# Windowed attention and two gated layers on one core: masks added on VectorE, weights rebased with one multiplication

## The chip, the cores and the metric

The kernel is one program on 1 core of a Trainium2 chip. The metric is the device time of one execution in microseconds (us).

## The reference, cut to what matters

Attention over 4 batches, 8 heads, 576 positions of 64 numbers; four heads see the last 32 positions, four see every fourth of the last 128. Two dense layers follow, over 2304 rows.

```python
scores = scale * np.matmul(q, k.transpose(0, 1, 3, 2))
scores = np.where(masks[None, :, :, :], scores, -1000000000.0)
scores = scores - np.max(scores, axis=-1, keepdims=True)
attn = np.exp(scores)
attn = attn / (np.sum(attn, axis=-1, keepdims=True) + 1e-09)
x = np.matmul(attn, v)                  # then laid out as 2304 x 512
h = x @ w_in                            # 512 -> 2048
x = (h * np.cos(h)) @ w_out             # 2048 -> 512
gate = 1.0 / (1.0 + np.exp(-(x @ w_gate)))   # 512 -> 1536
out = (gate * (x @ w_val)) @ w_out2     # 1536 -> 512
```

Inputs q, k, v are float32; the weights arrive as float64. The result is float32.

## The kernel before, in words

**Stages.** The first dense layer runs over 6 chunks of 384 rows and 16 slices of 128 hidden columns, 96 steps of 24 matmuls. Slices 0 to 7 go over all chunks first (steps 0 to 47), then slices 8 to 15. A float32 value is split into a rounded part and a remainder, and each product is three matmuls (`mm3`, lines 676 to 680). The second layer takes two chunks at a time, 36 sections, with seven block products for four (lines 960 to 1082). Attention works on 12 groups of 192 rows and 4 head pairs, 48 tiles, and runs beside steps 0 to 36.

**An attention tile** (`attn_tasks`, line 471). q and k are loaded (`load_qk`), turned on TensorE (`transp`), copied from PSUM on VectorE or ScalarE (`q_parts`, `k_parts`), and multiplied (`scores`). A plain tile has 3 blocks of 128 rows (two heads of 64) by 96 keys, a dilated tile 4 blocks of 96 rows by 80 keys. The mask reaches the scores by a matmul: the identity times a bfloat16 mask tile (`mp` or `md`, entries 0 or -2**33, lines 556 and 559) opens the PSUM group, and the score products add to it. `s_max` (line 568) takes each row's maximum. Tiles of the first two groups (`direct`) multiply the maximum by -scale (`s_neg`, line 576) and give it to the exponential as a bias, which then reads PSUM (line 584); the others subtract the maximum into SBUF first (`s_sub`, line 572), and the exponential reads SBUF (line 587). `s_norm` on GpSimd, a transposition, a copy, the product with V and a split into two parts follow. `band` (line 262) makes the masks on GpSimd at the start; a tile's first 32 keys are set by `head` on GpSimd.

**Weights** (`w_tasks`, line 309). A float64 tile of 128x512 is loaded (`wst`, two buffers) and made float32 with integer operations on its two 32-bit halves: `low` (ScalarE, line 332) scales the low half; `mag` clears the sign (VectorE, line 336, or ScalarE, line 340); `clamp` (line 344) takes the maximum with 2**-15; `shift` (line 347) moves left by 3 and masks; `top` (line 350) puts the top two bits back; `rnd` (line 360) adds the low part. `hi` (ScalarE, line 367) rounds to the matmul's format and `lo` (GpSimd, line 371) takes the remainder. Of 68 tiles, 16 belong to slices 0 to 7, 16 to slices 8 to 15, 36 to the second layer.

**The order of work** is written before the run by a planner (`Plan`, line 48): each task has an engine, a duration, inputs, buffers it takes and gives, a priority (the step at which it is due) and sometimes a second engine (`alt`). The planner steps through modelled time and gives each engine the ready task with the least priority; the chip's queues then hold that order. `port=True` keeps a task from running beside another such task (VectorE and GpSimd). `gate` holds a weight load until a step has begun: `W_GATE` names the first step and the step from weight to weight, for slices 8 to 15 and for the second layer. All loads are issued from SP's queue. Until step 0, TensorE is given small matmuls on an identity (`keep_warm`, line 1110).

Of the kernel before, what the change touches and what calls it, by code (L numbers as in the profile page):

```python
# [9 lines left out]
F32 = mybir.dt.float32  # L10
F32R = mybir.dt.float32r
BF16 = mybir.dt.bfloat16
I32 = mybir.dt.int32
# [9 lines left out]
NEG = -(2.0**33)  # L23
INV_2PI = 0.15915494309189535
TWO_PI = 6.283185307179586
HALF_PI = 1.5707963267948966
F64_MIN = 2.0**-15
# [12 lines left out]
W_GATE = (4.413, 1.646, 36.0, 1.7)  # L40
# [137 lines left out]
def windowed_attention_mlp_kernel(ctx, tc, q, k, v, w_in, w_out, w_gate, w_val, w_out2, out):  # L178
# [80 lines left out]
    mp = ac.tile([P, PB + 1, PW], BF16, name="mp")  # L259
# [14 lines left out]
    band(mp[:, 0, :], PW, True)  # L274
    band(mp[:, 1, :], PW, False)
    for i in range(2, PB + 1):
        POOL.tensor_copy(mp[:, i, :], mp[:, 1, :])
    for z in range(2):
        band(md[:, z, :], DW, z == 0)
# [29 lines left out]
    def w_tasks(i):  # L309
# [24 lines left out]
        def mag():  # L334
            st["c"] = wst.tile([P, DM], I32, tag="wc", name="wc")
            DVE.tensor_scalar(st["c"], st["raw"][:, :, 1], 0x7FFFFFFF, None, op0=ALU.bitwise_and)

        def mag_act():
            st["c"] = wst.tile([P, DM], I32, tag="wc", name="wc")
            ACT.activation(out=st["c"].bitcast(F32), in_=st["raw"][:, :, 1].bitcast(F32), func=AF.Abs)  # L340

        def clamp():
            c = st["c"].bitcast(F32)
            DVE.tensor_scalar(c, c, F64_MIN, None, op0=ALU.max)

        def shift():
            DVE.tensor_scalar(st["c"], st["c"], 3, 0x3FFFFFF8, op0=ALU.logical_shift_left, op1=ALU.bitwise_and)

        def top():
            DVE.scalar_tensor_tensor(st["c"], st["raw"][:, :, 1], -0x40000000, st["c"], op0=ALU.bitwise_and,  # L350
                                     op1=ALU.bitwise_or)
# [10 lines left out]
        def hi():  # L362
# [4 lines left out]
            ACT.activation(out=wt[key][:, 0, :], in_=st["c"].bitcast(F32), func=AF.Copy)  # L367
# [795 lines left out]
```

## Time and profile before

| | |
|---|---|
| median of 3 runs | 983.49 us (982.2 to 986.23) |
| profiled execution, its own time | 983.52 us |
| its span | 981.6 us |
| mean granted TensorE clock | 0.988 |
| instructions | 16366 |
| VectorE, mean of the 68 `top` / 68 `shift` / 68 `clamp` operations | 730 / 490 / 461 ns |
| ScalarE, mean of the 32 `hi` / 35 `mag` operations | 627 / 662 ns |

The span runs from the first to the last instruction of one profiled execution. Busy time is the union of an engine's instructions. Matmuls are pipelined and their listed lengths overlap, so TensorE's cost is read from starts. Idle time of an engine that nothing waits for costs nothing.

### The profile page before, as it was taken

To read this page: it belongs to the slowest core of one execution; us is meant where nothing else is said; L and a number is where in the kernel's file an instruction comes from. 1 tells how busy PE (TensorE), PEld (TensorE's weight loads), DVE (VectorE), ACT (ScalarE), POOL (GpSimd) and SP (SyncE) were. 2 spreads that over 40 slices of the span, in tenths; PEclk is the share of its full clock that TensorE was granted. 3 is DMA by queue.
4 is the path that set the end of the run, shared out by engine and by line. 5 is a ranking of instruction groups with operands and counts; after the bars stand their busy time and mean duration, and the time that the engine had idled before them with its cause. 6 is when DMAs were issued, how large, how long until landed. Compare 5 with 4: busy or idle time off the path is not lost.

```text
span 981.6 us, 16366 instructions
## 1 busy us (share of the span) xinstructions
PE 950.2 (97%) x6007; PEld 893.0 (91%) x6007; DVE 688.8 (70%) x1419; ACT 494.8 (50%) x1193; POOL 177.2 (18%) x228
## 2 busy tenths in 40 slices
PE   7889999999999999999999999999999999999996
PEld 6778889989999999999999989999999999999995
DVE  7789998978765987979899587657544645444443
ACT  5778888777665755665675443323312223221122
POOL 6334333223101332222213122100000000000000
PEclk9699999999999999999999999999999999999999
DMA  7565555455320566778758998785644544644441
GB/s 185 147 192 147 183 155 160 134 159 148 74 79 30 193 226 221 282 244 314 248 193 275 331 335 330 252 320 193 213 152 182 188 162 177 239 157 150 151 150 64
DMA packets 107759, 189.80 MB, mean 193 GB/s; under 512 B 56992, under 2 KB 91040, under 8 KB 100512
## 3 DMA queue, kind: packets, MB, share of 16 engines
q1 hardware_dynamic: 107680, 188.77, 56.7%
q8 instruction: 47, 0.77, 0.3%
q14 instruction: 32, 0.26, 0.1%
HBM read 139.98 MB, written 48.76 MB: 192 GB/s over the span
## 4 chain that ended last, share of the span: by engine, by line
PE 73%; DVE 12%; DMA 7%; ACT 6%; issue 2%; SPq 1%; ACTq 0%; DVEq 0%
PE acc L678 5%; PE ps_h L678 5%; PE oacc L1074 5%; PE oacc L1075 5%; PE oacc L1073 5%; PE acc L680 4%; PE acc L679 4%; PE ps_h L680 4%; PE ps_h L679 4%; PE ps_y L988 3%; PE ps_y L990 3%; PE ps_y L989 3%; PE ps_z L990 2%; PE ps_z L989 2%; PE ps_z L988 2%; PE ps_x L988 2%
## 5 line engine op out<-in xcount | busy, mean ns | idle before, releaser
L678 PE MATMUL acc<-gs,arena 128*128 128x384 f32 x384 | 135.3, 352 | 0.0
L678 PE MATMUL ps_h<-arena 128*128 128x384 f32 x384 | 131.8, 343 | 0.2 <-DVE u L738 0.2
L679 PE MATMUL ps_h<-arena 128*128 128x384 f32 x384 | 128.9, 336 | 0.0
L680 PE MATMUL ps_h<-arena 128*128 128x384 f32 x384 | 128.8, 335 | 0.0
L680 PE MATMUL acc<-gs,arena 128*128 128x384 f32 x384 | 128.7, 335 | 0.0
L679 PE MATMUL acc<-gs,arena 128*128 128x384 f32 x384 | 128.6, 335 | 0.0
L436 POOL TENSOR_TENSOR th<-tb,th 128x512 fp32r<-128x512 f32 (+1 forms) x48 | 60.4, 1272 | 185.4 <-ACT th L431 152.9
L1021 ACT ACTIVATE sg<-sg 128x384 f32<-128x384 f32 x36 | 18.9, 525 | 135.9 <-DVE sg L1017 135.9
L1073 PE MATMUL oacc<-arena 128*128 128x512 f32 x216 | 84.5, 391 | 2.4 <-DVE arena L1035 1.9
L1075 PE MATMUL oacc<-arena 128*128 128x512 f32 x216 | 85.5, 396 | 0.0
L1074 PE MATMUL oacc<-arena 128*128 128x512 f32 x216 | 85.5, 396 | 0.0
L728 ACT ACTIVATE r<-ps_h,q 128x384 int32<-128x384 f32 x96 | 55.4, 577 | 58.3 <-PE ps_h L680 55.8
L735 ACT ACTIVATE u<-u,half_pi 128x384 f32<-128x384 f32 x96 | 58.5, 612 | 38.5 <-DVE u L732 37.8
L1006 DVE TENSOR_TENSOR sg<-ps_y,s 128x384 f32<-128x384 f32 x36 | 20.0, 556 | 80.3 <-PE ps_y L990 80.3
L678 PEld LDWEIGHTS ps_h<-arena 128*128 128x128 f32 x384 | 72.4, 188 | 1.5 <-DVE u L738 0.5
L988 PE MATMUL ps_y<-arena 128*128 128x384 f32 x216 | 72.8, 337 | 0.7 <-DVE u L738 0.5
L678 PEld LDWEIGHTS acc<-gs,arena 128*128 128x128 f32 x384 | 72.2, 188 | 0.9
L990 PE MATMUL ps_y<-arena 128*128 128x384 f32 x216 | 72.9, 337 | 0.0
L989 PE MATMUL ps_y<-arena 128*128 128x384 f32 x216 | 72.8, 337 | 0.0
L679 PEld LDWEIGHTS ps_h<-arena 128*128 128x128 f32 x384 | 72.4, 189 | 0.2 <-POOL arena L371 0.2
L680 PEld LDWEIGHTS ps_h<-arena 128*128 128x128 f32 x384 | 72.4, 188 | 0.0
L679 PEld LDWEIGHTS acc<-gs,arena 128*128 128x128 f32 x384 | 72.3, 188 | 0.0
(137 smaller groups left out, 2340.1 us busy)
## 6 DMA issues: line engine op xcount, KB each, us to landing
arena<-wd SPq DMA_DIRECT2D x36, 1792.0 KB, 7.4
wd<-th SPq DMA_DIRECT2D x12, 1792.0 KB, 7.0
wst<-in_moe_w_out_dram SPq DMA_DIRECT2D x28, 512.0 KB, 4.2
wst<-in_moe_w_in_dram SPq DMA_DIRECT2D x16, 512.0 KB, 4.4
xd<-arena SPq DMA_DIRECT2D x4, 1536.0 KB, 6.2
wst<-in_moe_w_gate_dram SPq DMA_DIRECT2D x12, 512.0 KB, 4.3
wst<-in_moe_w_val_dram SPq DMA_DIRECT2D x12, 512.0 KB, 5.4
od<-oh SPq DMA_DIRECT2D x12, 512.0 KB, 6.9
```

What stands on the lines that cost most here:

```text
L436: POOL.tensor_tensor(out=t[:, 1, c], in0=wf[f][:, c].bitcast(F32), in1=t[:, 0, c].bitcast(F32), op=ALU.subtract)
L678: PE.matmul(ps, wh, xl, start=first, stop=False)
L679: PE.matmul(ps, wl, xh, start=False, stop=False)
L680: PE.matmul(ps, wh, xh, start=False, stop=last)
L728: ACT.activation(out=st["r"], in_=st["h"], func=AF.Identity, scale=INV_2PI, bias=q25)
L735: ACT.activation(out=st["u"], in_=st["u"], func=AF.Sin, scale=TWO_PI, bias=half_pi)
L988: PE.matmul(st[to], wh, xl, start=first, stop=False, **more)
L989: PE.matmul(st[to], wl, xh, start=False, stop=False, **more)
L990: PE.matmul(st[to], wh, xh, start=False, stop=kk == 1, **more)
L1073: PE.matmul(ps, ul, w[:, 0, :], start=f == 0, stop=False)
L1074: PE.matmul(ps, uh, w[:, 1, :], start=False, stop=False)
L1075: PE.matmul(ps, uh, w[:, 0, :], start=False, stop=f == F2 - 1)
```

## The change

Masks: no mask matmul; each score product starts its own PSUM region. For every block, one VectorE operation (`tensor_tensor_reduce`) adds the mask, multiplies by -scale, writes the result to SBUF and gives the row's minimum; that is 3 operations for a plain tile and 4 for a dilated one. The exponential then reads SBUF with scale -1 and the minimum as bias, in all tiles, and the scores' PSUM bank is free after the VectorE operations. `mp` shrinks from 4 blocks to 2, and GpSimd's two copies that filled it go.

Weights: `mag` becomes a multiplication of the high half, read as float32, by 2**-112, first choice ScalarE; `clamp` goes; `shift` loses its mask, `top` keeps one bit. `hi` may also run on VectorE.

Order: the first weight loads get a later priority than the first q and k load; k of the first group is issued from ScalarE's queue; `W_GATE` moves from 4.413 and 36.0 to 12.0 and 40.0. The planner's durations for the changed tasks change with them.

```diff
-F64_MIN = 2.0**-15
...
-W_GATE = (4.413, 1.646, 36.0, 1.7)
+W_GATE = (12.0, 1.8, 40.0, 1.7)
...
-    mp = ac.tile([P, PB + 1, PW], BF16, name="mp")
+    mp = ac.tile([P, 2, PW], BF16, name="mp")
...
-    band(mp[:, 0, :], PW, True)
-    band(mp[:, 1, :], PW, False)
-    for i in range(2, PB + 1):
-        POOL.tensor_copy(mp[:, i, :], mp[:, 1, :])
     for z in range(2):
+        band(mp[:, z, :], PW, z == 0)
         band(md[:, z, :], DW, z == 0)
...
-        def mag():
+        def mag(on_dve=False):
             st["c"] = wst.tile([P, DM], I32, tag="wc", name="wc")
-            DVE.tensor_scalar(st["c"], st["raw"][:, :, 1], 0x7FFFFFFF, None, op0=ALU.bitwise_and)
-
-        def mag_act():
-            st["c"] = wst.tile([P, DM], I32, tag="wc", name="wc")
-            ACT.activation(out=st["c"].bitcast(F32), in_=st["raw"][:, :, 1].bitcast(F32), func=AF.Abs)
-
-        def clamp():
-            c = st["c"].bitcast(F32)
-            DVE.tensor_scalar(c, c, F64_MIN, None, op0=ALU.max)
+            c, x = st["c"].bitcast(F32), st["raw"][:, :, 1].bitcast(F32)
+            if on_dve:
+                DVE.tensor_scalar(c, x, 2.0**-112, None, op0=ALU.mult)
+            else:
+                ACT.activation(out=c, in_=x, func=AF.Copy, scale=2.0**-112)
 
         def shift():
-            DVE.tensor_scalar(st["c"], st["c"], 3, 0x3FFFFFF8, op0=ALU.logical_shift_left, op1=ALU.bitwise_and)
+            DVE.tensor_scalar(st["c"], st["c"], 3, None, op0=ALU.logical_shift_left)
 
         def top():
-            DVE.scalar_tensor_tensor(st["c"], st["raw"][:, :, 1], -0x40000000, st["c"], op0=ALU.bitwise_and,
+            DVE.scalar_tensor_tensor(st["c"], st["raw"][:, :, 1], -0x80000000, st["c"], op0=ALU.bitwise_and,
...
-        def hi():
+        def hi(on_dve=False):
             if j < 0:
                 wt[key] = halves(at((i if i < NW else i - NW) * W_SZ, W_SZ))
             else:
                 wt[key] = late["oh"].tile([P, 2, DM], F32R, tag="oh", name="oh")
-            ACT.activation(out=wt[key][:, 0, :], in_=st["c"].bitcast(F32), func=AF.Copy)
+            if on_dve:
+                DVE.tensor_copy(wt[key][:, 0, :], st["c"].bitcast(F32))
+            else:
+                ACT.activation(out=wt[key][:, 0, :], in_=st["c"].bitcast(F32), func=AF.Copy)
...
-        add(("w_load", i), "sp", 1460, load, [], pr - 2 if j + 2 * F1 >= 2 * FN[0] else GS * (i / 4 - 6) + W_START, take=["raw"], lat=2200 if i < 2 * FN[0] else 3200, gate=gate,
+        add(("w_load", i), "sp", 1460, load, [], pr - 2 if j + 2 * F1 >= 2 * FN[0] else max(GS * (i / 4 - 6) + W_START, -GS * (A_LEAD + 1) - QK_LEAD + 0.1), take=["raw"], lat=2200 if i < 2 * FN[0] else 3200, gate=gate,
             after=[("w_load", i - 1)] if i else [])
         add(("w_low", i), "act", 520, low, [("w_load", i)], pr)
-        add(("w_mag", i), "dve", 335, mag, [("w_load", i)], pr, take=["wc"], port=True,
-            alt=("act", 520, mag_act, False))
-        add(("w_clamp", i), "dve", 335, clamp, [("w_mag", i)], pr, port=True)
-        add(("w_shift", i), "dve", 335, shift, [("w_clamp", i)], pr, port=True)
+        add(("w_mag", i), "act", 550, mag, [("w_load", i)], pr, take=["wc"], alt=("dve", 335, lambda: mag(True), True))
...
-            add(("w_hi", i), "act", 520, hi, [("w_rnd", i)] + extra, pr, take=["oh"] if j >= 0 else [])
+            add(("w_hi", i), "act", 520, hi, [("w_rnd", i)] + extra, pr, take=["oh"] if j >= 0 else [], alt=("dve", 335, lambda: hi(True), True))
...
+                queue = ACT if nm == "k" and g == 0 else SP
...
-                    SP.dma_start(
+                    queue.dma_start(
...
             ps = st["sc"] = pool.tile([P, n, w], F32, tag=ptag, name="ps_s")
-            if plain:
-                z = 0 if j == 0 else 1
-                PE.matmul(ps, identb, mp[:, z:z + n, :], start=True, stop=False)
-            else:
-                mk = md[:, 0 if j == 0 else 1, :].unsqueeze(1).to_broadcast([m, n, w])
-                PE.matmul(ps[:m], identb[:m, :m], mk, start=True, stop=False)
             for i in range(n):
                 if plain:
-                    PE.matmul(ps[:, i, :], qbp[:, i, :], kt[:, 64 * i:64 * i + w], start=False, stop=i == n - 1)
+                    PE.matmul(ps[:, i, :], qbp[:, i, :], kt[:, 64 * i:64 * i + w], start=True, stop=True)
                 else:
-                    PE.matmul(ps[:m, i, :], qbd[:, i, :], kt[:, i, :], start=False, stop=i == n - 1)
+                    PE.matmul(ps[:m, i, :], qbd[:, i, :], kt[:, i, :], start=True, stop=True)
 
         def s_max():
+            st["s"] = sp.tile([m, n, w], F32, tag="s", name="s", bufs=N_S)
             st["mx"] = smp.tile([m, n], F32, tag="mx", name="mx")
-            DVE.tensor_reduce(out=st["mx"], in_=st["sc"][:m], axis=AX.X, op=ALU.max)
-
-        def s_sub():
-            st["s"] = sp.tile([m, n, w], F32, tag="s", name="s", bufs=N_S)
-            DVE.tensor_tensor(out=st["s"], in0=st["sc"][:m], in1=st["mx"].unsqueeze(2).to_broadcast([m, n, w]),
-                              op=ALU.subtract)
-
-        def s_neg():
-            DVE.tensor_scalar(st["mx"], st["mx"], -scale, None, op0=ALU.mult)
+            for i in range(n):
+                mask = mp[:, 0 if j == 0 and i == 0 else 1, :] if plain else md[:, 0 if j == 0 else 1, :]
+                DVE.tensor_tensor_reduce(out=st["s"][:, i, :], in0=st["sc"][:m, i, :], in1=mask, scale=-scale, scalar=HUGE,
+                                         op0=ALU.add, op1=ALU.min, accum_out=st["mx"][:, i:i + 1])
...
-            ACT.activation(out=st["s"][:, i, :], in_=st["s"][:, i, :], func=AF.Exp, scale=scale,
+            ACT.activation(out=st["s"][:, i, :], in_=st["s"][:, i, :], func=AF.Exp, scale=-1.0, bias=st["mx"][:, i:i + 1],
...
-            add(("load_qk", half), "sp", 2200, load_qk, [], p1 - QK_LEAD, take=["qk"], lat=2200,
+            add(("load_qk", half), "sp", 2200 if g else 1100, load_qk, [], p1 - QK_LEAD, take=["qk"], lat=2200,
...
-        add(("scores", a), "pe", 760 * slow, scores, [("t_free", a)], p1, take=[bank, "s", "sm"])
-        add(("s_max", a), "dve", 370, s_max, [("scores", a)], p1)
-        direct = g < GPC
-        if direct:
-            add(("s_sub", a), "dve", 70, s_neg, [("s_max", a)], p1)
-        else:
-            add(("s_sub", a), "dve", 380, s_sub, [("s_max", a)], p1, give=[bank])
-        group = [("s_sub", a - ix % EG + i) for i in range(EG)] if g >= GPC else [("s_sub", a)]
+        add(("scores", a), "pe", 560 * slow, scores, [("t_free", a)], p1, take=[bank, "s", "sm"])
+        add(("s_max", a), "dve", 520 if plain else 600, s_max, [("scores", a)], p1, give=[bank])
+        group = [("s_max", a - ix % EG + i) for i in range(EG)] if g >= GPC else [("s_max", a)]
```

## Rows read from the trace of the kernel before

**Rows 1.** The first part of the page: busy time of each engine, its share of the span, number of instructions.

```profile
PE 950.2 (97%) x6007; PEld 893.0 (91%) x6007; DVE 688.8 (70%) x1419; ACT 494.8 (50%) x1193; POOL 177.2 (18%) x228
```

**Rows 2.** Busy time by stretch. Columns: stretch and its length (us), busy us (x instructions) of TensorE, its weight load, VectorE, ScalarE, GpSimd; then the granted TensorE clock, the DMA engines' share, GB/s.

```profile
0.00:62.00 62.00, 48.14 (x462) 43.01 (x462) 48.70 (x128) 42.55 (x144) 30.26 (x64) 0.85 0.68 189
62.00:310.00 248.00, 241.21 (x1990) 221.44 (x1989) 208.20 (x498) 185.61 (x542) 67.37 (x102) 1.00 0.45 130
310.00:540.00 230.00, 229.84 (x1326) 229.45 (x1326) 196.62 (x368) 139.81 (x262) 58.84 (x45) 1.00 0.67 234
```

**Rows 3.** The same table for the matmuls of line 678 alone (the first of three products, of both matrices of the first layer): TensorE, weight load, clock, DMA.

```profile
62.00:150.00 88.00, 35.53 (x95) 18.08 (x96) 0.99 0.53 154
150.00:280.00 130.00, 56.86 (x155) 29.14 (x155) 1.00 0.44 126
```

**Rows 4.** The same table for the mask matmuls, 62 to 310 us: first line 556 (plain heads), then line 559 (dilated heads).

```profile
62.00:310.00 248.00, 5.00 (x17) 1.64 (x17) 1.00 0.45 130
...
62.00:310.00 248.00, 5.29 (x17) 2.05 (x17) 1.00 0.45 130
```

**Rows 5.** The timeline of TensorE at three places: start (us), length (us), engine, line, operation, tiles, number merged, and in brackets the idle time before it and what ended it.

```profile
26.02 0.43 PE L559 MATMUL ps_s<-md,identb 96*96 96x320 bf16 x1 [1.62 <-ACT pt L546]
...
69.52 0.30 PE L556 MATMUL ps_s<-mp,identb 128*128 128x288 bf16 x1
69.65 0.58 PE L562 MATMUL ps_s<-ktp,qbp 128*128 128x96 f32 x4
...
153.22 0.34 PE L559 MATMUL ps_s<-md,identb 96*96 96x320 bf16 x1
153.39 0.83 PE L564 MATMUL ps_s<-ktd,qbd 128*96 128x80 f32 x8
```

**Rows 6.** Busy time of VectorE by stretch for single lines: two rows of line 568 (maximum), two of line 572 (subtraction), one of line 576 (sign and scale).

```profile
0.00:62.00 62.00, 6.09 (x13) 0.85 0.68 189
62.00:310.00 248.00, 16.23 (x35) 1.00 0.45 130
...
0.00:62.00 62.00, 2.28 (x5) 0.85 0.68 189
62.00:310.00 248.00, 16.34 (x35) 1.00 0.45 130
...
0.00:62.00 62.00, 3.79 (x8) 0.85 0.68 189
```

**Rows 7.** Groups of instructions by line and shape: line, engine, operation, tiles, out<-in, count | busy us, mean ns of one | idle before.

```profile
L738 DVE TENSOR_TENSOR u<-ps_h,u 128x384 f32<-128x384 f32 x96 | 53.0, 554 | 25.8 <-ACT u L735 24.8
...
L360 DVE CUSTOM_DVE_ANT_0 wc<-wst,wc 128x1024 uint16<-128x1024 uint16 x44 | 31.6, 719 | 0.2
...
L587 ACT ACTIVATION_READ_ACCUMULATOR s<-s 96x1 f32 x80 | 15.3, 191 | 0.0
...
L572 DVE TENSOR_TENSOR s<-ps_s,mx 128x288 f32<-128x288 f32 x20 | 9.0, 448 | 0.2
...
L594 DVE RECIPROCAL rs<-rs 128x3 f32<-128x3 f32 x24 | 4.0, 167 | 0.4
```

**Rows 8.** Busy time by stretch for single lines of the weight rebasing: two rows of line 344 (clamp, VectorE), two of line 336 (sign mask, VectorE), one of line 340 (sign mask, ScalarE).

```profile
0.00:62.00 62.00, 3.90 (x8) 0.85 0.68 189
62.00:310.00 248.00, 10.21 (x24) 1.00 0.45 130
...
0.00:62.00 62.00, 2.71 (x6) 0.85 0.68 189
62.00:310.00 248.00, 7.24 (x16) 1.00 0.45 130
...
62.00:310.00 248.00, 4.68 (x7) 1.00 0.45 130
```

**Rows 9.** The timelines of SP, GpSimd, TensorE, ScalarE and VectorE in the first 40 us, columns as in rows 5.

```profile
2.85 1.09 SPq L487 DMA_DIRECT2D k<-in_k_dram  x2
...
6.16 0.12 POOL L521 MEMSET ktp<- 128x32 f32 x1
...
7.75 0.34 PE L529 MATMUL ps_t<-ident,q 96*128 96x96 f32 x2
...
8.61 0.63 ACT L367 ACTIVATE arena<-wc 128x512 fp32r<-128x512 f32 x1 [1.41 <-DVE wc L360]
...
9.85 0.36 DVE L550 COPY ktp<-ps_t 128x192 f32<-128x192 f32 x1 [0.22 <-ACT qbp L546]
...
10.36 0.88 PE L562 MATMUL ps_s<-ktp,qbp 128*128 128x96 f32 x6 [1.15 <-DVE ktp L550]
...
39.58 0.67 PE L678 MATMUL ps_h<-arena 128*128 128x384 f32 x1
```

**Rows 10.** The timeline of SP's queue, 600 to 700 us.

```profile
610.64 0.38 SPq L325 DMA_DIRECT2D wst<-in_moe_w_gate_dram  x1
...
639.25 0.32 SPq L439 DMA_DIRECT2D wd<-th  x1
...
657.04 0.32 SPq L967 DMA_DIRECT2D arena<-wd  x1
```

**Rows 11.** Busy time by stretch, columns as in rows 2.

```profile
26.00:43.00 17.00, 16.30 (x114) 14.49 (x113) 13.29 (x35) 11.12 (x41) 7.16 (x10) 0.50 0.54 142
43.00:60.00 17.00, 12.09 (x123) 10.66 (x123) 14.61 (x37) 14.55 (x51) 5.35 (x8) 1.00 0.84 256
```

More of the change, by code (lines that the diff above doesn't have):

```diff
@@ L23 @@
 NEG = -(2.0**33)
+HUGE = 3.0e38
 INV_2PI = 0.15915494309189535
@@ L378, in w_tasks @@
             gate = min(W_GATE[2] + j * W_GATE[3], need - 8)
-        add(("w_load", i), "sp", 1460, load, [], pr - 2 if j + 2 * F1 >= 2 * FN[0] else GS * (i / 4 - 6) + W_START, take=["raw"], lat=2200 if i < 2 * FN[0] else 3200, gate=gate,
+        add(("w_load", i), "sp", 1460, load, [], pr - 2 if j + 2 * F1 >= 2 * FN[0] else max(GS * (i / 4 - 6) + W_START, -GS * (A_LEAD + 1) - QK_LEAD + 0.1), take=["raw"], lat=2200 if i < 2 * FN[0] else 3200, gate=gate,
             after=[("w_load", i - 1)] if i else [])
         add(("w_low", i), "act", 520, low, [("w_load", i)], pr)
-        add(("w_mag", i), "dve", 335, mag, [("w_load", i)], pr, take=["wc"], port=True,
-            alt=("act", 520, mag_act, False))
-        add(("w_clamp", i), "dve", 335, clamp, [("w_mag", i)], pr, port=True)
-        add(("w_shift", i), "dve", 335, shift, [("w_clamp", i)], pr, port=True)
+        add(("w_mag", i), "act", 550, mag, [("w_load", i)], pr, take=["wc"], alt=("dve", 335, lambda: mag(True), True))
+        add(("w_shift", i), "dve", 335, shift, [("w_mag", i)], pr, port=True)
         add(("w_top", i), "dve", 600, top, [("w_shift", i)], pr, port=True)
@@ L580, in s_exp @@
                 st["rs"] = smp.tile([m, n], F32, tag="rs", name="rs")
-            if direct:
-                if i == 0:
-                    st["s"] = sp.tile([m, n, w], F32, tag="s", name="s", bufs=N_S)
-                ACT.activation(out=st["s"][:, i, :], in_=st["sc"][:m, i, :], func=AF.Exp, scale=scale,
-                               bias=st["mx"][:, i:i + 1], accum_out=st["rs"][:, i:i + 1])
-                return
-            ACT.activation(out=st["s"][:, i, :], in_=st["s"][:, i, :], func=AF.Exp, scale=scale,
+            ACT.activation(out=st["s"][:, i, :], in_=st["s"][:, i, :], func=AF.Exp, scale=-1.0, bias=st["mx"][:, i:i + 1],
                            accum_out=st["rs"][:, i:i + 1])
@@ L650, in attn_tasks @@
         add(("t_free", a), None, 0, nothing, [("q_out", a, 0), ("q_out", a, 1), ("k_out", a)], p1, give=[bank])
-        add(("scores", a), "pe", 760 * slow, scores, [("t_free", a)], p1, take=[bank, "s", "sm"])
-        add(("s_max", a), "dve", 370, s_max, [("scores", a)], p1)
-        direct = g < GPC
-        if direct:
-            add(("s_sub", a), "dve", 70, s_neg, [("s_max", a)], p1)
-        else:
-            add(("s_sub", a), "dve", 380, s_sub, [("s_max", a)], p1, give=[bank])
-        group = [("s_sub", a - ix % EG + i) for i in range(EG)] if g >= GPC else [("s_sub", a)]
+        add(("scores", a), "pe", 560 * slow, scores, [("t_free", a)], p1, take=[bank, "s", "sm"])
+        add(("s_max", a), "dve", 520 if plain else 600, s_max, [("scores", a)], p1, give=[bank])
+        group = [("s_max", a - ix % EG + i) for i in range(EG)] if g >= GPC else [("s_max", a)]
         for i in range(n):
             add(("s_exp", a, i), "act", 255, lambda i=i: s_exp(i), group,
-                GS * (g - A_LEAD + (ix - ix % EG) / KD) - EXP_LEAD + ix * 1e-3 + i * 1e-4, table="exp", after=[("s_exp", a, i - 1)] if i else [],
-                give=[bank] if direct and i == n - 1 else [])
+                GS * (g - A_LEAD + (ix - ix % EG) / KD) - EXP_LEAD + ix * 1e-3 + i * 1e-4, table="exp", after=[("s_exp", a, i - 1)] if i else [])
         add(("s_eps", a), "dve", 70, s_eps, [("s_exp", a, i) for i in range(n)], p2)
```

## The prediction

> **What bounds the kernel now.** I read the page first: TensorE is busy for 97% of the span, VectorE for 70%, ScalarE for 50% [rows 1]. An average does not say where, so the table by stretch came next [rows 2]. From 310 to 540 us TensorE idles 0.2 us of 230; it is the bound there, and no edit takes a matmul out of that stretch or of the second layer behind it. From 62 to 310 us, where attention runs beside the first layer, it idles 248.0 - 241.2 = 6.8 us, and VectorE is busy 208.2 of 248, ScalarE 185.6. From 0 to 62 us it idles 13.9 us, part of its busy time is warm-up matmuls that compute nothing, and the granted clock averages 0.85. That stretch is a relay between VectorE (48.7 us busy) and ScalarE (42.6), which copy q, k and probabilities, with TensorE waiting in turn.
>
> The middle stretch hides a second loss. One line's matmuls tell the pace: L678 runs 95 times in 62 to 150 (0.926 us each) and 155 times in 150 to 280 (0.839 us each) [rows 3]. Attention per step is about the same in both, so the early part is 95 x 0.087 = 8 us behind the later pace. I count 6 us of it as open to a faster VectorE, the rest to the low clock near 60 us.
>
> **Mask matmuls, removed.** 48 go; 34 of them run after 62 us [rows 4], 14 before. Their listed length is not what they cost, since matmuls overlap: the one at 153.22 is listed with 0.34 us and the next starts at 153.39. By starts, a dilated mask holds TensorE 0.17 us and a plain one (69.52 to 69.65) 0.13 [rows 5]. 34 x 0.13 to 0.17 is 4.4 to 5.8 us; I take 0.16, that is 5.4 us, in a stretch where TensorE is the bound. The cover that goes: the mask matmul runs while the copies of q and k land. Late next is the first score matmul, which waits for the same copies; at the lowest, with all that cover turned into waiting, the saving is nothing. Starting each product fresh instead of adding to the mask changes no duration that I can see.
>
> **VectorE's maximum, subtraction and sign, replaced.** Removed in 0 to 310: L568 22.3 us, L572 18.6, L576 3.8, in all 44.7 us [rows 6]. Added: 72 operations of 128x96 and 96 of 96x80 that read PSUM and a mask and also give a minimum. The trace has none of these, so I bound one. Below: two-input VectorE operations of 384 and 288 elements take 554 and 448 ns, 1.1 ns an element, which gives 240 ns at 96 and 220 at 80. Above: the only custom VectorE operation in the trace, L360, takes 719 ns for 1024 half-words, three times what the slope gives [rows 7]. I take the slope, because those operations read the same PSUM tiles on the same engine: 72 x 0.240 + 96 x 0.220 = 38.4 us, 6.3 us less than what goes. At 719 ns it would be 120.8 us, 76 more than what goes.
>
> The Trainium skill speaks against this part: VectorE: DVE Perf Modes, section "Two Vector instructions with no wait between them", says that an operation which also writes out its accumulator is two instructions, the second one an accumulator read. On VectorE no row shows one. By that rule 168 more small operations would be added.
>
> As a mechanism of this kernel, an accumulator read on VectorE would be as long as its smallest row, L594 with 167 ns: 168 x 0.167 = 28.1 us more, 66.5 in place of 38.4. ScalarE's exponentials do run with such a partner, of 191 ns [rows 7].
>
> **Weights.** The clamp L344 goes: 14.1 us in 0 to 310, of them 3.9 in the first 62. The sign mask L336 ran on VectorE 22 times there (9.9 us) and else on ScalarE (L340, 0.67 us each); the multiplication's first choice is ScalarE, so up to 22 x 0.67 = 14.7 us go to ScalarE [rows 8]. There it waits for the same load as the low half's scaling beside it, so nothing new is held up behind it but by its length. Shift, top and add keep their counts; the rounding copy may now go to VectorE, where ScalarE is late. VectorE over 0 to 310 is thus 256.9 - 6.3 - 14.1 - 9.9 = 226.6 us, ScalarE 228.2 + 14.7 = 242.9; both are under 80% of 310. By the accumulator rule VectorE would be at 254.7, hardly any relief. After 310 the lighter weights shorten VectorE only, and TensorE has no idle time to give back: nothing.
>
> **First loads.** The issues of the first q and k end at 3.94 us behind two weight loads; they are transposed at 7.75, and the first scores start at 10.36, after the key copy at 9.85, which stood behind the first weights on VectorE [rows 9]. With q ahead of the weights on SP and k on ScalarE's queue, both end issuing near 1.8 us, 2.1 earlier; transposes come near 5.6. The first weights, issued 1 us later, reach VectorE behind the key copy instead of ahead of it. The key tile also waits for GpSimd's memset of its head at 6.16, behind the masks, where two small copies go. Scores then start near 6.8: 3.5 us earlier. The price: four DMA issues of 0.5 us on ScalarE, in a time when it waits for data anyway; SP reaches the first V load and the third weight 2 us sooner. The weights are not late for it: the first is rounded at 8.61, the first h matmul runs at 39.58.
>
> **0 to 62 us, rest.** VectorE there: -6.1 - 2.3 - 3.8 - 3.9 - 2.7 (L336) + 11.2 (7 tiles of each kind) = -7.6 us; ScalarE +6 x 0.67 = +4.0 [rows 6, 8]. If the two share the work evenly the relay is 1.8 us shorter. With the start: 5.3 us, between 0 (the relay waits elsewhere) and 14.
>
> **62 to 310 us.** VectorE: -16.2 - 16.3 - 10.2 - 7.2 + 27.2 = -22.7 of 208.2, and the later gate moves the first weights of the second half from step 5 to step 12, out of the early part, where the pace is low. I take 4 of the 6 us above, between 0 and 9. The gate of the second layer's weights, four steps later, costs nothing: the last gate weight's old gate is step 92.1 of the 96 of the first layer, its new one 96.1, passed with the second section of the next, and it was loaded only at 610.64. Its buffers and not the gate hold it; the block is saved at 639.25 and read at 657.04 [rows 10].
>
> **Sum.** 983.5 (the profiled execution: span 981.6 and 1.9 around it; the median shown is 983.49) - 5.4 - 5.3 - 4 = 968.8, **969 us**. Own range 960 to 977.
>
> **Rivals.** (a) Only the mask matmuls count: ScalarE, which takes the rebasing, becomes what the relay waits for. For it: ScalarE is at 14.6 of 17 us in 43 to 60; against: at 11.1 of 17 before that [rows 11]. 983.5 - 5.4 = 978 us. (b) More is won: in 26 to 43 us the granted clock is 0.50, the lower of the two levels, 1.2 GHz, and TensorE is busy 16.3 of 17 us, so it is the bound there at half speed [rows 11]; the clock fell when TensorE had just waited 1.62 us, up to 26.02 [rows 5]. Without that fall 16.3 / 2 = 8 us more go: 961, and with the whole middle loss 957. (c) Slower: the new operation is dear on VectorE. At a mean of t us VectorE holds 188.2 + 168 t in 0 to 310: above 0.41 there is no relief. At today's share (256.9 of 310, 83%) a t of 0.45 needs 318 us, and the 8 more eat the masks' 5.4 and most of the start's 3.5: from there on it is slower. At 0.50 it needs 329, that is 983.5 + 19 - 9 = about 993. (d) The accumulator read exists: t = 0.40, so only masks and start count, 983.5 - 8.9 = 975. (The page behind this one is VectorE: DVE Perf Modes of the Trainium skill, the section named above.) (e) The change does not do for time what it says: the copies of q and k become the wait that the mask matmul covered, and the order comes out no better: 982.
>
> **How the numbers follow.** Forecast 0.58; (a) 0.12; (b) 0.12; (c) 0.07; (d) 0.06; (e) 0.05. What a measurement can tell from no change is 0.5%, 4.9 us: faster means below 978.6. The forecast, (b), (d) and half of (a), which sits on the line, are faster, less a few hundredths for orders of work that come out worse: 0.76. The other half of (a), (e) and part of those orders are the same, 0.15. (c) and the rest are slower, 0.09. The range 954 to 985 holds all but (c) and the ends.
>
> **What would show it.** Right: no L556 or L559 on TensorE; the new VectorE rows near 0.23 us; first scores near 7 us; less than 6.8 us of idle TensorE in the middle stretch; L678's early pace near 0.84. Wrong: new rows of 0.45 us or more, a longer stretch at clock 0.50, or TensorE waiting on ScalarE's rebasing.

## The result: 0.5% slower, and the profile after

The changed kernel takes 988.02 us (median of 16 runs, 984.30 to 994.06), the kernel before 983.30 in the runs beside it: a ratio of 1.0051 [1.0030, 1.0072]. The forecast was 969, the range ended at 985. The profiled execution took 987.88 us with a span of 986.1 at a mean granted clock of 0.987. Two medians below, 992.84 and 974.48, each count one stray execution of over 2000 us (992.27 and 974.29 without it); the ratios leave it out.

The first part of the page, as in [rows 1]:

```profile
PE 946.4 (96%) x5922; PEld 889.1 (90%) x5922; DVE 659.8 (67%) x1604; ACT 501.0 (51%) x1180; POOL 175.8 (18%) x226
```

Busy time by stretch, columns and stretches as in [rows 2]:

```profile
0.00:62.00 62.00, 47.19 (x431) 41.93 (x433) 43.63 (x194) 41.38 (x142) 26.88 (x63) 0.86 0.64 165
62.00:310.00 248.00, 234.78 (x1903) 214.71 (x1900) 194.69 (x637) 189.76 (x529) 68.30 (x102) 0.99 0.46 132
310.00:540.00 230.00, 229.19 (x1335) 228.44 (x1334) 189.54 (x357) 139.41 (x259) 55.99 (x42) 1.00 0.65 234
```

VectorE lost work as it should: 238.3 us from 0 to 310 after 256.9. Yet in the middle stretch TensorE's idle time doubled, from 6.8 to 13.2 us, and ScalarE got 4.2 us busier. After 310 us little changes but the offset. The pace of the first layer, in the rows that answer to [rows 3] (line 655 now), is what it was, 95 and 155 matmuls, where the early part was to catch up:

```profile
62.00:150.00 88.00, 32.30 (x95) 18.13 (x96) 0.98 0.50 145
150.00:280.00 130.00, 52.09 (x155) 29.10 (x155) 1.00 0.44 127
```

The offset itself arises late. ScalarE's `r` operation runs once a step of the first layer, 96 times in all. Its 35th and 39th run, before and then after:

```profile
283.98 0.58 ACT L728 ACTIVATE r<-ps_h,q 128x384 int32<-128x384 f32 x1 [1.62 <-PE ps_h L680]
...
306.13 0.58 ACT L728 ACTIVATE r<-ps_h,q 128x384 int32<-128x384 f32 x1 [1.62 <-PE ps_p L602]
```

```profile
284.13 0.58 ACT L703 ACTIVATE r<-ps_h,q 128x384 int32<-128x384 f32 x1 [1.62 <-PE ps_h L655]
...
310.16 0.58 ACT L703 ACTIVATE r<-ps_h,q 128x384 int32<-128x384 f32 x1 [1.62 <-PE ps_h L655]
```

At the 35th the two kernels are level: what the change saves is eaten by idle time. Then, at the end of attention, the changed kernel falls 4.0 us behind. TensorE, which had no idle time there, waits 2.1 us, and the mean granted clock is 0.91 (before, then after):

```profile
290.00:310.00 20.00, 20.00 (x162) 18.60 (x162) 11.61 (x28) 13.99 (x49) 2.73 (x4) 1.00 0.25 79
```

```profile
290.00:310.00 20.00, 17.90 (x127) 16.39 (x126) 13.94 (x31) 12.99 (x42) 5.57 (x6) 0.91 0.35 112
```

The groups by line and shape (columns as in [rows 7]) show the instructions that are new or longer:

```profile
L568 ACT ACTIVATE s<-s,mx 96x80 f32<-96x80 f32 x96 | 33.3, 349 | 0.0
...
L568 ACT ACTIVATE s<-s,mx 128x96 f32<-128x96 f32 x72 | 26.1, 364 | 0.1
...
L562 DVE CUSTOM_DVE_ANT_0 s<-ps_s,md 96x80 f32<-96x80 f32 x96 | 17.1, 231 | 2.5 <-PE ps_s L554 2.5
...
L562 DVE CUSTOM_DVE_ANT_0 s<-ps_s,mp 128x96 f32<-128x96 f32 x72 | 14.5, 250 | 4.9 <-PE ps_s L552 4.7
...
L562 DVE DVE_READ_ACCUMULATOR2_ANT mx<- 96x1 f32 x96 | 7.5, 78 | 0.0
...
L562 DVE DVE_READ_ACCUMULATOR2_ANT mx<- 128x1 f32 x72 | 5.9, 81 | 0.1
```

The same groups of the kernel before, for its exponentials without a bias operand (line 587) and with one (line 584):

```profile
L587 ACT ACTIVATE s<-s 96x80 f32<-96x80 f32 x80 | 20.4, 258 | 0.0
...
L587 ACT ACTIVATE s<-s 128x96 f32<-128x96 f32 x60 | 16.3, 275 | 0.1
...
L584 ACT ACTIVATE s<-ps_s,mx 96x80 f32<-96x80 f32 x16 | 5.0, 317 | 2.8 <-DVE mx L576 2.8
...
L584 ACT ACTIVATE s<-ps_s,mx 128x96 f32<-128x96 f32 x12 | 3.9, 336 | 0.7 <-DVE mx L576 0.7
```

The new VectorE operation is 10 ns longer than forecast. The exponential is 90 ns longer than line 587's, with the row's minimum as a bias operand; exponentials with such an operand were there before the change, in line 584, and the prediction did not price it. In the timeline of ScalarE the starts of neighbours stand 0.37 us apart:

```profile
209.35 0.38 ACT L568 ACTIVATE s<-s,mx 128x96 f32<-128x96 f32 x1
209.63 0.19 ACT L568 ACTIVATION_READ_ACCUMULATOR s<-s,mx 128x1 f32 x1
209.72 0.36 ACT L568 ACTIVATE s<-s,mx 128x96 f32<-128x96 f32 x1
```

And the start, where 3.5 us were to be won. The chain of waits up to 12 us (start, length, what):

```profile
1.71 6.20 DMA wst<-in_moe_w_in_dram
...
7.93 2.07 DMA k<-in_k_dram
...
10.01 0.34 ACT ktp L542
...
10.48 1.57 PE ps_s L552 x6
```

The first transposes do come early, at 3.52 us after 7.75, but the first scores start at 10.48 after 10.36 [rows 9]. ScalarE's timeline shows what stands between:

```profile
5.09 0.34 ACT L542 ACTIVATE qbp<-ps_t 64x192 f32<-64x192 f32 x1 [1.75 <-PE ps_t L525]
7.93 2.03 ACTq L483 DMA_DIRECT2D k<-in_k_dram  x2
10.01 0.33 ACT L542 ACTIVATE ktp<-ps_t 128x192 f32<-128x192 f32 x1 [4.57 <-DMA k<-in_k_dram]
```

The key loads of the second half are issued by ScalarE too. They stand in its queue ahead of the first key copy and go out at 7.93, just after the first weights have landed (1.71 + 6.20 = 7.91), so ScalarE stands idle for 4.57 us before the copy. The trace tells why. The loads signal their landing by semaphores (counters that an instruction can wait for); the first 14 loads share eight of them, 100 to 107, and the two held issues wait for 104 and 105, which the first two weight loads had before them. They go out at 7.93 and 9.64, each 0.02 us after its weight load has landed. It is the program's own wait.

### The profile page after: what moved, and what is told of

Its sections match the earlier page's. It is cut to its first block, busy times and chain, and to the rows that moved or that the text cites. A ratio compares the mean times of both kernels' runs of the same rounds, so it can differ in the third digit from the quotient of the medians.

```text
span 986.1 us, 16400 instructions
## 1 busy us (share of the span) xinstructions
PE 946.4 (96%) x5922; PEld 889.1 (90%) x5922; DVE 659.8 (67%) x1604; ACT 501.0 (51%) x1180; POOL 175.8 (18%) x226
## 4 chain that ended last, share of the span: by engine, by line
PE 82%; ACT 8%; DVE 6%; DMA 2%; issue 1%; SPq 0%; ACTq 0%; DVEq 0%
PE ps_h L653 6%; PE ps_h L655 6%; PE ps_h L654 6%; PE acc L653 6%; PE acc L655 5%; PE acc L654 5%; PE oacc L1049 5%; PE oacc L1048 5%; PE oacc L1050 5%; PE ps_y L965 4%; PE ps_y L963 4%; PE ps_y L964 4%; ACT s L568 4%; PE ps_z L965 3%; PE ps_z L964 3%; PE ps_z L963 2%
## 5 line engine op out<-in xcount | busy, mean ns | idle before, releaser
L713 DVE TENSOR_TENSOR u<-ps_h,u 128x384 f32<-128x384 f32 x96 | 53.2, 556 | 32.6 <-ACT u L710 31.5
L653 PEld LDWEIGHTS acc<-gs,arena 128*128 128x128 f32 x384 | 72.3, 188 | 2.3 <-DVE o L782 1.1
L653 PEld LDWEIGHTS ps_h<-arena 128*128 128x128 f32 x384 | 73.3, 191 | 0.4
L654 PEld LDWEIGHTS ps_h<-arena 128*128 128x128 f32 x384 | 73.3, 191 | 0.0
L655 PEld LDWEIGHTS ps_h<-arena 128*128 128x128 f32 x384 | 73.2, 191 | 0.0
```

What stands on the lines that cost most here:

```text
L653: PE.matmul(ps, wh, xl, start=first, stop=False)
L654: PE.matmul(ps, wl, xh, start=False, stop=False)
L655: PE.matmul(ps, wh, xh, start=False, stop=last)
```

## The experiments

The expectations name theories by letters. A: the bias operand's 90 ns per exponential. B: the order that the planner makes of the changed tasks. C: VectorE's accumulator reads. D: the later gate. E: the first loads. P: the length that the planner assumes for an exponential, 255 ns in both kernels (for line 587's it was measured at 258 and 275). Two kernels with the same order on every engine are called a matched pair.

**The bias operand, taken out and put in.** Each run makes a matched pair with its parent. The first leaves out that the row's maximum is taken off.

```diff
-ACT.activation(..., func=AF.Exp, scale=-1.0, bias=st["mx"][:, i:i + 1],
+ACT.activation(..., func=AF.Exp, scale=-1.0,
```

> The changed kernel with one operand less: the exponential takes no bias, so the row minimum is still computed but not used, and the exponentials are those of the scores without the row maximum taken off. Order of work on every engine the same as in the changed kernel. Theory A (the bias operand makes each exponential 0.09 us longer, 349 and 364 ns against 258 and 275 before, and the cosines of the first layer stand behind each batch): exponentials fall to about 260 and 275 ns, TensorE's idle time from 62 to 310 us falls from 13 us to 7 or less, total 977 to 981, below the kernel before. Rival B (the new order of work or the later weight gate is what loses): exponentials get shorter, but the total stays at 986 to 988. Rival C (the accumulator reads on VectorE, 168 of 80 ns, are the loss): total stays at 985 to 988, with VectorE's rows unchanged.

Measured: 979.77 us, 0.9962 [0.9948, 0.9977] of before, 8.3 us under the change. The second gives the kernel before a tile of zeros as bias (line 587):

```diff
-ACT.activation(..., func=AF.Exp, scale=scale,
+ACT.activation(..., func=AF.Exp, scale=scale, bias=zb[:m, :],
...
```

> The kernel before with one operand more: its exponentials that read SBUF (140 of 168) get a bias of zero from a tile, the arithmetic stays the same and so does the order of work on every engine. Theory A: each of the 140 becomes about 0.09 us longer (12.6 us of ScalarE in all) and the total goes from 983.3 to 989 to 993. Rivals B and C: the total moves by less than 2 us, since nothing of the order, the gate or VectorE is touched.

Measured: 993.0 us, 1.0098 [1.0083, 1.0113]. The groups of the two runs, first without the operand in the change, then with it in the kernel before:

```profile
L568 ACT ACTIVATE s<-s 96x80 f32<-96x80 f32 x96 | 24.4, 258 | 0.0
...
L568 ACT ACTIVATE s<-s 128x96 f32<-128x96 f32 x72 | 19.5, 273 | 0.1
```

```profile
L587 ACT ACTIVATE s<-s,zb 96x80 f32<-96x80 f32 x80 | 27.8, 353 | 0.0
...
L587 ACT ACTIVATE s<-s,zb 128x96 f32<-128x96 f32 x60 | 21.8, 367 | 0.1
```

The operand costs 91 to 95 ns an instruction, with the same source and destination; so PSUM was not what made line 584 long. (With the operand, line 584's reads of PSUM, 317 and 336 ns, are even shorter than the 353 and 367 from SBUF.) The Trainium skill states it: ScalarE: Activation LUTs, section "What ACT_TABLE_LOAD costs", gives about 93 ns for each pointer operand of an activation. These rows agree. The table by stretch says where it goes: TensorE's idle time from 62 to 310 us is 248 - 239.30 = 8.7 us without the operand in the change, 14.5 with it in the kernel before (6.8 without). Theory A had 7 or less for the first:

```profile
62.00:310.00 248.00, 239.30 (x1936) 219.68 (x1935) 196.78 (x639) 180.66 (x532) 67.65 (x100) 0.98 0.45 127
```

```profile
62.00:310.00 248.00, 233.50 (x1913) 212.35 (x1913) 203.50 (x488) 192.65 (x535) 67.20 (x103) 1.00 0.46 130
```

**The parts alone.** The mask part undone in the change; then the mask part alone in the kernel before.

```diff
-                    PE.matmul(ps, ..., start=True, stop=True)
+                PE.matmul(ps, identb, mp[:, z:z + n, :], start=True, stop=False)
+                    PE.matmul(ps, ..., start=False, stop=i == n - 1)
...
```

> The changed kernel with its mask part undone: mask matmuls, maximum and subtraction as before; weights, gate and first loads as changed. Theory A (the mask part brings its loss with the bias operand, the other parts bring little): 980 to 984. Rival B (order, gate and weights lose): 988 or more, since the mask matmuls' 5 us come back as well. Rival C: as A, 980 to 984, since the accumulator reads go too.

Measured: 987.42 us, 1.0035 [1.0021, 1.0049]: not the 980 to 984 of theory A, and just short of B.

> The kernel before with the mask part of the change alone: weights, gate and first loads as before. Theory A: the saving on TensorE (5 us) is outweighed by the longer exponentials, 985 to 990, with VectorE not relieved by the weights. Rival B: 977 to 980, since only the other parts lose. Rival C: 985 to 990 as well; the run with the bias operand added alone tells it from A.

Measured: 985.65 us, 1.0020 [1.0006, 1.0034]. So weights, gate and loads lost 3.5 us on their own, and the masks 1.7, where the sum had 9.3 us for the start and the middle stretch and 5.4 for the mask matmuls. The weights alone, in the kernel before:

> The kernel before with the weight conversion alone changed (one multiplication in place of magnitude and clamp, the shift and the sign's operation without their masks, the rounding copy allowed on VectorE too); masks, exponentials, gate and loads as before. The prediction's count (VectorE relieved by some tens of conversions between 62 and 310 us, TensorE's idle time there mostly a wait for ScalarE): 980 to 983.5 us. Theory B (a planner that is free to put the rounding copy on either engine fills VectorE where TensorE waits for it): 984.5 to 988 us.

Measured: 992.84 us, 1.0078 [1.0056, 1.0099], worse than either theory said. VectorE has 196.6 us of work in the middle stretch instead of 208.2, and TensorE idles 13.5 us instead of 6.8; four more stretches of 3.4 us, between 85 and 151 us, run at the lower of the two clock levels (1.2 GHz). Less work on an engine bought nothing. How much of the loss is the waiting in the new order and how much the lower clock was not tried apart; four such stretches account for at most 4 x 1.7 = 6.8 us.

**Gate and first loads**, one line of the change at a time. The gate's edit makes the planner write another order; the queue's leaves the order as it is.

```diff
-W_GATE = (12.0, 1.8, 40.0, 1.7)
+W_GATE = (4.413, 1.646, 36.0, 1.7)
```

> The changed kernel with the four numbers of the weight gate as before (first weight of the second half at step 4.4 instead of 12, second layer at 36 instead of 40). Theory D (the later gate crowds the rebasing of the second half's weights into the end of attention, where the changed kernel falls 2.6 us back between steps 36 and 38, as does the run with the masks undone): total falls by 2 to 4 us to 984 to 986. Rival E (what is lost besides the bias operand lies in the first loads): total within 1.5 us of 988.

Measured: 986.88 us, 1.0027 [1.0014, 1.0041], 1.1 under the change; the two intervals overlap. The 4 us at the end of attention are gone (between the 35th and 39th run of `r` it loses 0.3 us against the kernel before), but it gets there 2.9 us late.

```diff
-                queue = ACT if nm == "k" and g == 0 else SP
+                queue = ACT if nm == "k" and half == 0 else SP
```

> The changed kernel with the second pair of k loads of the first group issued from SP again; the first pair stays on ScalarE's queue, and the order of work elsewhere is the same. In the changed kernel that second pair waits in ScalarE's queue until the first weight loads have landed (issued at 7.93 and 9.64 us) and the key copy behind it waits 4.57 us. Theory E: the key copy runs near 5.5 us, the first scores near 6 instead of 10.48, and the total falls by 1 to 4 us to 984 to 987. Rival D: the first scores come earlier, but the gain is lost on the way, and the total stays within 1 us of 988.

Measured: 985.98 us, 1.0017 [1.0004, 1.0031], 2.0 under the change, a matched pair. The same edit with the mask part undone, again a matched pair:

> The masks, the subtraction and the exponentials are those of the kernel before; the weight chains, their gate and the first loads are those of the change, but only the first half's key loads are issued by ScalarE, the second half's by SyncE. Theory E (what ate the gain of the first loads is the second half's key issue that stands on ScalarE's queue ahead of its copies): the run without this edit was 3.4 us over the kernel before, the same edit on the whole change took 2.0 us off, so 980 to 983 us, below or level with the kernel before, with the first step some 4 us early. Theory B (the weights' new chains and the order planned for them lose on their own, whatever the loads do): 986 to 988 us, with the loss at the same places as without this edit.

Measured: 984.38 us, 0.9998 [0.9985, 1.0012]: between the two expectations. Its first scores start at 7.42 us in TensorE's timeline:

```profile
7.42 1.44 PE L561 MATMUL ps_s<-ktp,qbp 128*128 128x96 f32 x6
```

That is 2.9 us earlier than [rows 9], and 2.8 earlier than without the edit (10.17); the total is 3.0 lower. Most of what the edit wins at the start is still there at the end. And both cures in the order of the change, without the operand:

> The changed kernel with both edits: no bias operand of the exponentials (the row maximum is not taken off) and the second k loads from SP; the order of work is that of the changed kernel. If the two causes add: 979.8 less what the second k loads give alone, that is 976 to 979. If the first loads give nothing that lasts: 979 to 981.

Measured: 976.16 us, 0.9928 [0.9915, 0.9940], 3.6 under its pair without the operand: the two causes add.

**One VectorE instruction per tile** in place of three or four pairs, added to the run before (the maximum is neither found nor taken off; `mp` has its 4 blocks and GpSimd its two copies again):

```diff
...
-            for i in range(n):
-                DVE.tensor_tensor_reduce(..., op0=ALU.add, op1=ALU.min, accum_out=st["mx"][:, i:i + 1])
+            DVE.scalar_tensor_tensor(st["s"], st["sc"][:m], -scale, mask, op0=ALU.mult, op1=ALU.add)
...
-        add(("s_max", a), "dve", 520 if plain else 600, s_max, ...)
+        add(("s_max", a), "dve", 390, s_max, ...)
```

> As the run with both edits, and the mask is added by one VectorE operation a tile (288 or 320 elements, near 450 to 480 ns), which scales and adds and takes no minimum, in place of three or four with their accumulator reads (0.8 to 0.9 us a tile). The row maximum is not taken off. The planner sees the shorter duration, so the order changes. If VectorE's load in the first 310 us matters still: 2 to 5 us below the run with both edits, 972 to 977. If not: within 1.5 us of it.

Measured: 985.91 us, 1.0023 [1.0009, 1.0036], a miss. The next run leaves the planned lengths 520 and 600 as they were, which makes it a matched pair with the run before:

> As the earlier run with one VectorE instruction per score tile (row maximum neither found nor taken off, and the second key load on SyncE), but with the planner's lengths left as the change has them, so that every engine's order is that of the run without bias and with the second key load on SyncE. Theory B (the earlier run's 985.9 came from its re-planned order, not from the instruction): 974 to 977 us, at or a little below the 976.2 of the run whose order it has. Rival (one instruction over four tiles releases the exponentials later than four short ones do): 980 us or more, with TensorE's idle time between 62 and 310 us above 8.7 us.

Measured: 974.48 us, 0.9898 [0.9878, 0.9919]. The instruction wins some 2 us; the order planned with its shorter length costs 11.4. The accumulator reads (theory C) are thus no more than a part of some 2 us. The idle time that the rival names was not read.

**The planner's length of an exponential.** First the whole change, with one number of the planner's table changed. The instructions stay the same, but the plan gives some 20 tasks to VectorE that were ScalarE's (copies of q, k and probabilities, five `gs`), and the order is another:

```diff
-            add(("s_exp", a, i), "act", 255, ...
+            add(("s_exp", a, i), "act", 350, ...
```

> The whole change, with the planner told that an exponential takes 350 ns in place of 255, about what it was measured to take. Theory A (the 94 ns of the bias are true work in a stretch where ScalarE's exponentials release TensorE, and no order hides them): 986 to 990 us. Theory B (the loss is an order that was planned with the wrong length): 980 to 983.5 us. Since the order is planned anew, a change within 2 us of 988 tells little beyond that planning does not recover the loss.

Measured: 981.36 us, 0.9966 [0.9953, 0.9979], 6.7 under the change. The same number in three more kernels: the change without the operand, and the kernel before without and with it.

> As the whole change planned with 350 ns (981.4 us), in the same order on every engine, with the exponential's bias operand left out (the row maximum not taken off). Theory P (an order planned with the true length hides most of the 94 ns): 979 to 981.5 us. Theory A (the 94 ns are on TensorE's path in any order): 972 to 975 us, some 8 us lower, as in the order planned with 255.

Measured: 978.91 us, 0.9946 [0.9934, 0.9959], at the lower edge of theory P.

> The kernel before with not one instruction changed, only planned as if an exponential of the 258 ns sort took 350. Theory P (a planned length that is wrong costs time because the order serves a kernel that isn't there): 986 to 992 us. Rival (a longer planned length is only caution, and the order hardly cares): 982 to 985 us. If it comes out below 982, the planner's figures are no model of the chip and e2's gain is luck of an order as much as truth.

Measured: 990.64 us (985.77 to 993.67), 1.0061 [1.0038, 1.0083].

> The kernel before with a zero bias operand on its exponentials (993.0 us in the order planned with 255 ns), planned with 350 instead. Theory P: 984 to 987 us, most of the 9 us back. Theory A: 991 to 994 us, nothing back.

Measured: 992.15 us (986.97 to 995.06), 1.0077 [1.0055, 1.0099]. Theory A's range, though not for its reason: the operand adds only 1.5 us to its matched parent, which is not clear of noise, but the order costs what it saves. And the mask part alone:

> The kernel before with the mask part of the change alone, planned with 350 ns for an exponential. If the mask term of the prediction holds once the length is known: 977 to 980 us (984 less 5.4, a couple of us either way for the order). If the 94 ns per exponential eat the term in any order: 984 to 988 us.

Measured: 978.09 us, 0.9941 [0.9919, 0.9963], 7.6 under the same instructions planned with 255.

| us | planned 255 | planned 350 |
|---|---|---|
| change, no operand | 979.77 | 978.91 |
| change | 988.02 | 981.36 |
| before | 983.3 to 984.3 | 990.64 |
| before, operand added | 993.0 | 992.15 |
| masks alone | 985.65 | 978.09 |

Down a column stands the operand's price in a fixed order: 8.3 and about 9 us where the plan knew nothing of it, 2.5 and 1.5 where it did (part of the 2.5 goes with the granted clock, at the median 0.987 with the operand and 0.992 without). The middle stretch says the same. First the change planned with 350, then its pair without the operand:

```profile
62.00:310.00 248.00, 241.72 (x1959) 222.49 (x1960) 197.84 (x665) 186.86 (x519) 70.83 (x103) 0.98 0.44 128
```

```profile
62.00:310.00 248.00, 241.65 (x1965) 222.83 (x1964) 196.96 (x663) 174.52 (x517) 67.79 (x102) 0.98 0.44 126
```

ScalarE's work differs by 12.3 us, TensorE's idle time not at all (6.3 and 6.4 us). In the kernel before planned with 350 it is 9.9 us, and 10.2 with the operand. Across a row stands the price of an order. The true length wins 6.7 and 7.6 us in the change and in the masks alone, and a length that is not its own costs the kernel before 6.4 us; but in the other two rows, one with the true length and one with the wrong one, 0.9 us is all that it moves. So a better number in the table does not by itself make a better order. The kernel before loses its 6.4 us early, and much of them goes with the clock: its runs take 985.77 us at a mean granted clock of 0.989 and 992.0 to 993.7 at 0.974 to 0.976. In the profiled one the first 62 us ran at 0.74:

```profile
0.00:62.00 62.00, 53.29 (x466) 49.09 (x466) 47.99 (x123) 37.60 (x132) 27.02 (x62) 0.74 0.67 180
```

**The best version that keeps the whole computation**: the change, 350 ns, and the second key load on SyncE.

> The whole change, planned with 350 ns for an exponential, and the second half's key loads issued by SyncE. Theory A+E (two separate losses, each with its own cure: the planned length took 6.7 us off, the key issue 2.0): 978 to 980 us. Rival (the order planned anew moves by more than the second cure is worth): anything from 976 to 986 us.

Measured: 977.52 us, 0.9929 [0.9916, 0.9942], faster than both kernels, and 3.8 under its matched pair, the change planned with 350, whose first scores start at 9.96. Its own first scores start at 6.58 us and its middle stretch idles 5.8:

```profile
6.58 1.54 PE L552 MATMUL ps_s<-ktp,qbp 128*128 128x96 f32 x6
```

```profile
62.00:310.00 248.00, 242.18 (x1959) 222.98 (x1959) 196.16 (x654) 185.54 (x516) 65.86 (x100) 0.99 0.44 125
```

> The whole change planned with 350 ns, the second key load on SyncE (977.5 us), and the weights' due times of the kernel before. If the new due times cost of themselves: 975.5 to 977 us. If they only moved the order: anything from 975 to 983 us, and no more is to be read from it than the size of that spread.

Measured: 978.18 us, 0.9936 [0.9911, 0.9961], the same, in another order: the new gate as such costs nothing that can be seen.

## Why the prediction was wrong, step by step

**The step that failed first** is the one that was not there. The part on VectorE's maximum, subtraction and sign prices what VectorE loses and gets, and the weights part sets ScalarE at "228.2 + 14.7 = 242.9"; neither counts that 140 exponentials get a bias operand. 140 x 0.09 = 12.6 us of ScalarE's time were missing. The rows that could have priced it stood in the trace, 317 and 336 ns with the operand beside 258 and 275 without; the prediction shows neither. In the order of the change the operand costs 8.3 us (the first pair above); by which waits it reaches TensorE was not followed.

**The mask matmuls**, 5.4 us: plausible, but not shown. Planned with the true length the mask part wins 984.2 - 978.1 = 6.1 us against the kernel before, but 12.6 against the kernel before planned with the same 350, and with 255 it loses 1.7; no two of these have one order. TensorE's busy time over the whole run, by the pages, falls from 950.2 us [rows 1] to 947.6 with the masks alone and to 945.1 with them planned with 350, and from 949.9 with the masks undone to 946.4 in the change.

**The new VectorE operation**: 231 and 250 ns were measured for 220 and 240. The accumulator read of rival (d) is there, as the Trainium skill states (VectorE: DVE Perf Modes, section "Two Vector instructions with no wait between them"), but with 80 ns where the estimate from the smallest row was 167, and the listed lengths overlap. VectorE's timeline:

```profile
202.01 0.25 DVE L562 CUSTOM_DVE_ANT_0 s<-ps_s,mp 128x96 f32<-128x96 f32 x1
202.19 0.08 DVE L562 DVE_READ_ACCUMULATOR2_ANT mx<- 128x1 f32 x1
202.19 0.25 DVE L562 CUSTOM_DVE_ANT_0 s<-ps_s,mp 128x96 f32<-128x96 f32 x1
```

A pair takes 0.18 us from start to start. As merged busy time line 562 takes two rows:

```profile
0.00:62.00 62.00, 9.78 (x103) 0.86 0.64 165
62.00:310.00 248.00, 22.27 (x236) 0.99 0.46 132
```

Together 32.1 us in place of 44.7 [rows 6]; the forecast was 38.4, and rival (d), by the 167 ns of the smallest row, 66.5. Rival (c) falls, and so does (d), whose read is there but not its price.

**The weights**: the multiplication did not go to ScalarE. It ran on VectorE 21 times in the first 310 us (9.9 us, as the sign mask did [rows 8]) and on ScalarE 9 times, and the rounding copy went to VectorE 11 times (4.6 us). So VectorE is at 238.3 us, not 226.6. That relief bought no time either: "4 of the 6 us" for 62 to 310 did not come in the change, whose TensorE idles 6.4 us more there; the best version wins 1 us of idle time.

**Rivals (a), (b) and (e).** For (a) the rebasing would have had to go to ScalarE, and it did not. For (b) the clock would have had to stay up: over the first 62 us its mean is 0.86 after 0.85. (e), 982, is nearest, and its "order comes out no better" came true; the wait that it names, the scores' for the copies of q and k, did not grow (4.0 us from 62 to 310 before, 2.0 after, by TensorE's list of waits).

**First loads**: "four DMA issues of 0.5 us on ScalarE, in a time when it waits for data anyway" is the second step that failed. Two of the four stood ahead of the key copy and were held by a semaphore until the first weights had landed. In four matched pairs, issuing them from SyncE takes off 2.0, 3.0, 3.6 and 3.8 us, where the first scores start 2.8 to 3.9 us earlier: an early start is kept, mostly, as long as the order is the same. With SyncE they start at 6.58 us where 6.8 was forecast.

**What the two failed steps explain.** With both taken out in the order of the change the time is 976.16 us: 11.9 of the 19.2 us between 988.0 and 968.8. The other 7 were not traced to one step. The terms for the start, the rest of the first 62 us and the middle stretch, 9.3 us in all, gave nothing that can be seen beside the masks: masks alone, planned with 350 (978.1), come out within 0.6 us of the best version. Where their gain is lost was not settled: the run with masks undone and the second key loads on SyncE is 10.7 us ahead of the kernel before at step 2 and 2.3 us behind at step 8 (starts of `r`), and in between lie a stretch of low clock from 94.4 to 101.2 us and the planned order.

**The gate**, "costs nothing": nothing clear of noise. Putting the old gate back wins 1.1 us in the change and loses 0.7 in the best version, each time with another order. The later gate alone is also not what costs 4 us at the end of attention: the change planned with 350 has the same gate and loses 0.2 us there.

**The order of work** carried "a few hundredths" of the chances. A planned length alone moved four sets of instructions by 6.4 to 11.4 us (the kernel before, the change, the masks alone, the one instruction per tile), more than the whole diff did, and two others by 0.9. That is the term that the range lacked. Whether the order costs by its waits or by the clock that falls in them stays open.

## What to carry to other kernels

When an edit moves a value from an instruction into an operand of another, price the receiving instruction too: find a row of the same operation with that operand, even if something else differs in it. When the order of work is planned from a table of lengths, a wrong length for the changed instructions can hide what an edit is worth: the same masks came out 1.7 us behind the kernel before or 6.1 us ahead of it, by one number in the planner. Measure those instructions and try the true number, but do not count on it: it won some 7 us in two kernels and 0.9 in a third. When a load is held, find the semaphore that its issue waits for before you blame the queues. And compare instructions in matched orders, since a new order by itself moves this kernel by more than most edits.

## What the runs showed of the hardware

A bias operand on a ScalarE exponential of 80 or 96 elements costs 91 to 95 ns, a third more than without it. With the operand, a source in PSUM took 317 and 336 ns where one in SBUF took 353 and 367. A VectorE operation with an accumulator output and its read are listed with 0.25 and 0.08 us, but such pairs start every 0.18 us. A load issued from a compute engine's queue holds up that engine's work behind it while the issue waits for a semaphore: 4.57 us of idle time on ScalarE at the start of the change, until a weight load issued by SyncE had landed.
